# Loading and scoring the first four heads in pairs, and three smaller changes of order

One change to a tuned attention-and-mixer kernel: the first four heads of q and k are loaded, cast, transposed and scored as two pairs, each with its own score sets; V comes behind the next q and k in the load queue; the identity matrix is built first; and some operations get finer urgency levels.

## The chip, the cores and the metric

One core of one Trainium2 chip. The metric is the device time of one execution in microseconds (us). Times are medians of several runs. The kernel before and a variant always ran on the same chip in alternation. "Clock" is the mean clock granted to TensorE, 1.0 being full speed.

## The reference

```python
# q, k, v: (8 batches, 8 heads, 576 positions, 64); the mask is causal in blocks of 64
scores = scale * q @ k^T                        # masked, softmax over the last axis
x = (softmax(scores) @ v), heads side by side   # (8, 576, 512)
h = relu(x^T @ w_tok1) @ w_tok2                 # token mixing: 576 -> 256 -> 576
u = x + h^T
out = u + relu(u @ w_ch1) @ w_ch2               # channel mixing: 512 -> 1536 -> 512
```

## The kernel before

The kernel writes every operation into a list with an engine, a planned cost, the operations it waits for and a priority; its own list scheduler plans the whole run with these costs and then emits the instructions of each engine in the planned order. The order on an engine is thus fixed when the kernel is built, from planned times.

The first four heads: k and q, 128 partitions (four heads of 32 rows each), in two column halves, one on SyncE's queue and one on ScalarE's. Casts and transposes take all 128 partitions at once. Everything after these loads comes through GpSimd's queue.

```python
def load_qk(b, hg, after=[]):
    first = b == 0 and hg == 0
    ...
    for n, (src, raw, dst) in enumerate(((k, kraw[i], kT[i]), (q, qraw[i], qT[i]))):
        ...
        for f, (k0, k1) in enumerate(parts):             # two column halves
            if first:
                def emit_load(o, ...):
                    queue = nc.sync if o.engine == "SP" else nc.scalar
                    queue.dma_start(out=st[:, D * k0 : D * k1], in_=hbm[:, D * k0 : D * k1])
                ld = P.add(("SP", "ACT")[f % 2], 0.45, emit_load, (), -1e4 + n, xfer=(k1 - k0) * 0.1)
                ...
                ld = P.add(EVAC, {"ACT": act_cost(w), "DVE": dve_cost(w)}, emit_cast, [ld], -1e4 + 2 + n)
            ...                                          # then a transpose on VectorE
```

Products of zeros are there to keep TensorE's clock up while there is no work: 16 at the start, and up to 110 small ones that the scheduler drops into whatever TensorE idle time it plans between 5 and 20 us.

```python
def raise_clock():
    def emit(o, bank=bank):
        for _ in range(WARM):                            # WARM, KEEP = 16, 110
            nc.tensor.matmul(out=bank_of(bank), lhsT=zeros[:, 0:128], rhs=zeros, start=True, stop=True)
    P.add("PE", WARM * 0.36, emit, pads["zeros"], -1e6, take=[(BANK, bank)], give=[bank])
    for n in range(KEEP):
        def emit(o, bank=bank):
            nc.tensor.matmul(out=bank_of(bank)[:, 0:256], lhsT=zeros[:, 0:128], rhs=zeros[:, 0:256], ...)
        P.add("PE", 0.11, emit, pads["zeros"], 1e6, take=[(BANK, bank)], give=[bank],
              at=5.0 + 0.12 * n, until=20.0, quick=True)
```

A score set multiplies k by q for several heads. A head uses 32 of the array's 128 rows (`r = slice(32 * h, 32 * h + 32)`), so a set for two heads has half of the rows in use (the timelines show such a product as `32*128`, one on all rows as `128*128`). Before the change the very first set takes all four heads at once; all others take pairs.

The softmax here doesn't subtract the row's maximum and nothing guards it: scores larger than these inputs give would overflow.

Of the kernel before, what the change touches and what calls it, by code (L numbers as in the profile page):

```python
# [149 lines left out]
def kernel(  # L150
# [96 lines left out]
    def init_tiles():  # L247
        def fill(engine, key, prio, *parts):
            for t, value in parts:
                def emit(o, t=t, value=value):  # L250
                    (nc.vector if engine == "DVE" else nc.gpsimd).memset(t, value)

                pads.setdefault(key, []).append(P.add(engine, 0.17, emit, (), prio))

        for i, t in enumerate(kT):
            fill("DVE", ("kT", i), -1e4 + i, (t[:, S:640, :], 0.0))
        for i in range(2):
            fill(
                "DVE", ("v", i), -60 + 20 * i,
                (v1[i][64:128, 4, :, :], 0.0),  # L260
                (v1[i][:, 0:4, :, 64:65], 1.0),
                (v1[i][0:64, 4, :, 64:65], 1.0),
            )
            fill("DVE", ("e", i), -70, (e_sb[i][:, :, 1536:1600], 0.0))
            fill("DVE", ("et", i), -70, (et_sb[i], 0.0))
            fill("DVE", ("um", i), -70, (um_sb[i], 0.0))
        fill("DVE", "zeros", -1e5, (zeros, 0.0))
        fill("DVE", "w1", -70, (w1_sb[64:128, 4, :], 0.0), (w1o_sb[0:64, :], 0.0))
        fill("DVE", "w2", -70, (w2_sb[:, :, S:640], 0.0))

        def emit(o):
            make_identity(nc, ident)

        pads["ident"] = [P.add("POOL", 0.9, emit, (), 5.5)]

    def raise_clock():

# [30 lines left out]
    def cast(o, dst, src):  # L308
        if o.engine == "ACT":
            nc.scalar.copy(dst, src)  # L310
        else:
            nc.vector.tensor_copy(dst, src)

    def load_qk(b, hg, after=[]):
        i = (2 * b + hg) % 3
        first = b == 0 and hg == 0
        prio = 10 * b + 4 * hg - (100 if b == 0 else 0)
        parts = ((0, NB // 2), (NB // 2, NB))
        done = []
        for n, (src, raw, dst) in enumerate(((k, kraw[i], kT[i]), (q, qraw[i], qT[i]))):  # L320
            hbm = src[b, 4 * hg : 4 * hg + 4].rearrange("h (p k) d -> (h p) (k d)", p=32)
            raw2 = raw.rearrange("p k d -> p (k d)")

            st = stage[0][:, 1152 * n : 1152 * (n + 1)]
            raw_war = reuse(("raw", n, i))
            T_war = reuse(("T", n, i))
            loads = []
            if not first:
                def emit_load(o, hbm=hbm, raw2=raw2):
                    nc.gpsimd.dma_start(out=raw2, in_=hbm)  # L330

                loads = [P.add("POOL", 0.66, emit_load, raw_war, prio + n, xfer=8 * 0.191)]
            for f, (k0, k1) in enumerate(parts):
                if first:
                    def emit_load(o, k0=k0, k1=k1, hbm=hbm, st=st):
                        queue = nc.sync if o.engine == "SP" else nc.scalar
                        queue.dma_start(out=st[:, D * k0 : D * k1], in_=hbm[:, D * k0 : D * k1])

                    ld = P.add(("SP", "ACT")[f % 2], 0.45, emit_load, (), -1e4 + n, xfer=(k1 - k0) * 0.1)

                    def emit_cast(o, k0=k0, k1=k1, raw2=raw2, st=st):
                        cast(o, raw2[:, D * k0 : D * k1], st[:, D * k0 : D * k1])

                    w = D * (k1 - k0)
                    ld = P.add(EVAC, {"ACT": act_cost(w), "DVE": dve_cost(w)}, emit_cast, [ld], -1e4 + 2 + n)
                    reads(("g", 0), ld)
                    loads = [ld]

                def emit(o, raw2=raw2, dst=dst, k0=k0, k1=k1):
                    nc.vector.transpose(  # L350
                        dst[:, 0:S, :]
                        .rearrange("p s e -> p (s e)")
                        .bitcast(I32)
                        .rearrange("p (a k) -> p k a", k=NB)[:, k0:k1],
                        raw2.bitcast(I32).rearrange("p (k a) -> p k a", k=NB)[:, k0:k1],
                    )

                op = P.add("DVE", 0.02 + 32 * (k1 - k0) * 0.00185, emit, loads + T_war + after, prio + 0.1 * n, urgent=-(b > 1))
                reads(("raw", n, i), op)
                done.append(op)  # L360
        return done

    def load_v(b):

        t = v1[b % 2]
        war = reuse(("v", b % 2))
        staged = b < 2
        done = [[], []]
        for hg in range(2) if b == 0 else (None,):
            hs = slice(0, H) if hg is None else slice(4 * hg, 4 * hg + 4)  # L370
            nh = hs.stop - hs.start
            for J in range(5):
                p = 128 if J < 4 else 64
                st = stage[1][0:p, DM * J : DM * (J + 1)].rearrange("p (h d) -> p h d", h=H)[:, hs]
                dst = t[0:p, J, hs, 0:64]

                def emit(o, J=J, p=p, hs=hs, dst=st if staged else dst):
                    src = v[b, hs, 128 * J : 128 * J + p, :].rearrange("h p d -> p h d")
                    nc.gpsimd.dma_start(out=dst, in_=src)  # L379

                prio = (10 * b + (0, 5.7, 6)[min(b, 2)] if b else (-95.5, 2)[hg]) + 0.01 * J
                sw = reuse(("gs", J)) if staged and b else [] if staged else war
                op = P.add("POOL", 0.2 + 0.075 * nh, emit, sw, prio, xfer=p * nh / 16 * (0.0175 if staged else 0.0145))
                if staged:
                    def emit(o, st=st, dst=dst):
                        cast(o, dst, st)

                    op = P.add("DVE", dve_cost(64 * nh, 2), emit, [op] + war, 10 * b + 2 if b else -94)
                    reads(("g", 1), op)
                    reads(("gs", J), op)  # L390
                for g in (0, 1) if hg is None else (hg,):
                    done[g].append(op)
        return done
# [190 lines left out]
    def first_attention(ready, v_ready):  # L584
# [3 lines left out]
        for j in range(4):  # L588
# [6 lines left out]
            for n, s in enumerate((2, 1, 0)):  # L595
                width = sum(w for _, _, _, w in SETS[s])
                parts = tuple((hg,) + r for r in SETS[s])
                dst = e[:, hs, 512 * s : 512 * s + width]
                if j == 0 and n == 0:

                    note = {}
                    early = [{}, {}]
                    op = score_set(
                        0, parts, range(4), ready[hg], prio - 0.05, [(SC, note)] + [(BANK, x) for x in early]
                    )
                if j == 1 and n == 0:
                    these = []
                    for h, x in zip(heads, early):
                        def emit(o, h=h, x=x, e=e):
                            nc.scalar.activation(e[:, h, 1024:1536], bank_of(x), EXP, scale=scale)  # L610

                        these.append(P.add("ACT", act_cost(512), emit, [op0], prio, give=[x], urgent=2))
                else:
                    if j or n:
                        note = {}
                        op = score_set(0, parts, heads, ready[hg], prio + 0.1 * n, [(SC, note)])
                    else:
                        op0 = op
                    these = [exp(dst, width, op, note, prio + 0.1 * n, urgent=2)]
                if n == (1 if j else 2):  # L620
                    tails = first_tail(hg, heads, [op] + ready[hg], prio + 0.1 * n + 0.05)
                exps += these
                for c in MASKS[s]:
                    exps.append(mask(e, c, hs, these, prio, urgent=1))
            for h in heads:
                deps = exps + v_ready[hg] + pad + pads["e", hg]
                done.append(head_out(0, 4 * hg + h, deps, -2900 + j, tails[h], urgent=1))
        return done

    def attention(b, ready, v_ready):  # L630
# [82 lines left out]
    def first_uT(x_done, a_done, w2_ready):  # L713
# [3 lines left out]
        for m in range(NDM):  # L717
# [24 lines left out]
                        stop=(t == NDT - 1),  # L742
                    )

            op = P.add("PE", mm_cost(512, 2), emit, [a_done[m], first] + w2_ready, -2700 + m, urgent=1)
            reads(("a", 0), op)
            reads(("x", 0), op)

# [4 lines left out]
                else:  # L753
                    nc.vector.tensor_copy(uT[0][:, :, m, :], ps)

            done.append(P.add(EVAC, evac_cost(512), emit, [op], -2700 + m, give=[bank], urgent=1))
        return done

    def token_mix(b, x_done, w1_ready, w2_ready):
# [9 lines left out]
        u_done, done, um_done = [], [], []  # L769
        if b == 0:  # L770
            a_all = [
                token_up(0, slice(128 * m, 128 * m + 128), (0, 1), x_done[2 * m : 2 * m + 2], [], w1_ready, -2800 + m, 1)
                for m in range(NDM)
            ]
            done = first_uT(x_done, a_all, w2_ready)
# [245 lines left out]
    warm_up()  # L1021
    qk = {}
    vv = {}
    qk[0, 0] = load_qk(0, 0)
    qk[0, 1] = load_qk(0, 1, qk[0, 0])
    vv[0] = load_v(0)
    init_tiles()
    raise_clock()
# [3 lines left out]
    for b in range(B + 1):  # L1032
        if b < B:
            if b > 0:
# [1 line left out]
                    qk[b, hg] = load_qk(b, hg)  # L1036
                vv[b] = load_v(b)
            x_done[b] = (
                attention(b, (qk[b, 0], qk[b, 1]), vv[b]) if b else first_attention((qk[0, 0], qk[0, 1]), vv[0])
            )  # L1040
        if b > 0:
            p = b - 1
# [44 lines left out]
```

## Time and profile before

| | before |
|---|---|
| time, median of 3 | 308.61 us (308.06 to 310.44) |
| profiled run: time, span, clock | 309.31, 307.5 us, 1.0 |
| TensorE busy | 98% of the span |
| first exponential on ScalarE | 10.58 us |
| first channel-up product | 29.04 us |

The prediction below shows the lines that carry the argument. Two more are needed later. The first is TensorE's timeline at the start (start, duration, engine, line, operation, output from input, shapes, count, and in brackets the idle time ahead and what ended it):

```profile
1.20 5.60 PE L282 MATMUL mm<-zeros 128*128 128x512 bf16 x16 [1.20 <-DVE zeros L251]
6.63 1.58 PE L289 MATMUL mm<-zeros 128*128 128x256 bf16 x13
9.91 0.32 PE L465 MATMUL sc<-qT,kT 32*128 32x320 bf16 x2 [1.70 <-DVE qT L350]
```

Thirteen of the small zero products stand between the first sixteen and the first scores. TensorE is idle 1.70 us all the same, because q landed later than planned. The profile's clock row misses one thing here: the first sixteen start 0.42 us apart up to 5.2 us and 0.22 us apart after it, so TensorE begins at half speed, and the trace's clock records begin only at 5.2 us. All 15 traces begin like this, up to some point between 3.84 and 6.86 us. "Clock 1.0" and "never" below leave this start out.

The second is the chain of waits, here two long pieces of it (start, duration, what):

```profile
29.10 2.71 PE mm L879 x12
...
291.20 12.99 PE mm L963 x72
```

They are the first and the last long stretch of channel mixing; their starts are the marks for the comparison.

### The profile page before, as it was taken

The numbers are of one execution on the slowest core, as the hardware profiler recorded it, in microseconds if no ns is written. First come the engines' busy times: TensorE is split into PE (matmuls) and PEld (weight loads), VectorE is DVE, ScalarE is ACT, GpSimd is POOL, SyncE is SP. The second block draws the span as 40 slices with busy tenths as digits, with TensorE's granted clock in tenths as the row PEclk, the third lists the DMA queues.
The fourth block names the chain that finished last, engine by engine and source line by source line (L and its number), as shares of the span: only waits on it lengthen the run. The fifth ranks groups of instructions, "written<-read, shape, count | busy, mean of one in ns | idle before, by whom it ended". The sixth has DMA issues, their size and how long they took to land.

```text
span 307.5 us, 7211 instructions
## 1 busy us (share of the span) xinstructions
PE 300.9 (98%) x3036; PEld 162.0 (53%) x3036; DVE 158.0 (51%) x396; ACT 165.6 (54%) x235; POOL 62.3 (20%) x96
## 2 busy tenths in 40 slices
PE   8799999999999999999999999999999999999995
PEld 3466447464564545545545556555445644545643
DVE  5677738997875859866749634362033012011022
ACT  3796774657775576785566784515405602604600
POOL 7865435620511241320050000000000000000000
PEclk9999999999999999999999999999999999999999
DMA  7999999997695599995292005112321312111013
GB/s 237 187 183 208 214 216 184 230 192 175 85 138 81 113 186 119 137 94 54 85 79 87 2 18 53 70 68 54 60 76 71 68 68 80 24 68 70 0 34 137
DMA packets 55872, 33.13 MB, mean 108 GB/s; under 512 B 43872, under 2 KB 46048, under 8 KB 55840
## 3 DMA queue, kind: packets, MB, share of 16 engines
q0 software_dynamic: 35808, 18.52, 45.8%
q1 hardware_dynamic: 19744, 13.57, 17.1%
q10 hardware_dynamic: 288, 0.59, 0.5%
q8 instruction: 23, 0.38, 0.5%
q14 instruction: 9, 0.07, 0.1%
HBM read 35.85 MB, written 9.44 MB: 147 GB/s over the span
## 4 chain that ended last, share of the span: by engine, by line
PE 93%; DMA 2%; ACT 2%; DVE 1%; issue 1%; ACTq 0%
PE mm L963 31%; PE mm L879 28%; PE mm L512 10%; PE sc L465 9%; PE mm L693 6%; PE mm L787 5%; PE mm L906 4%; DMA gT<-in_q_dram 2%; DVE qT L350 1%; ACT e_sb L484 1%; PE mm L737 1%; ACT uT L855 0%; PE mm L955 0%; PE mm L722 0%; ACT qraw L310 0%
## 5 line engine op out<-in xcount | busy, mean ns | idle before, releaser
L484 ACT ACTIVATE e_sb<-sc 128x1024 bf16<-128x1024 f32 x95 | 92.5, 1027 | 33.2 <-PE sc L465 32.4
L879 PE MATMUL mm<-uT,wc_sb 128*128 128x512 bf16 x384 | 88.8, 380 | 0.2 <-ACT uT L855 0.2
L963 PE MATMUL mm<-wc_sb,gT 128*128 128x512 bf16 (+1 forms) x396 | 88.6, 373 | 0.0
L679 ACT ACTIVATE gT<-mm 128x512 bf16<-128x512 f32 x75 | 44.9, 598 | 64.7 <-PE mm L879 63.7
L879 PEld LDWEIGHTS <-wc_sb 128*128 128x128 bf16 x384 | 42.2, 114 | 39.7 <-issue 3.7
L963 PEld LDWEIGHTS <-gT 128*128 128x128 bf16 x396 | 37.0, 98 | 41.8 <-issue 3.6
L988 DVE TENSOR_TENSOR o_sb<-mm,u_sb 128x512 f32<-128x512 f32 (+1 forms) x29 | 19.5, 672 | 63.2 <-PE mm L963 63.2
L465 PE MATMUL sc<-qT,kT 32*128 32x320 bf16 (+4 forms) x744 | 35.5, 281 | 1.9 <-DVE qT L350 1.7
L512 PEld LDWEIGHTS <-e_sb 128*128 128x128 bf16 x896 | 30.8, 97 | 8.1 <-issue 4.3
L512 PE MATMUL mm<-v,e_sb 128*128 128x65 bf16 x896 | 33.2, 193 | 0.0
L540 DVE TENSOR_TENSOR x_sb<-mm,rinv 128x320 bf16<-128x320 f32 x64 | 30.5, 488 | 1.8
L379 POOL DMA_DIRECT2D v<-in_v_dram x30 | 25.3, 861 | 29.0 <-PE sc L465 21.6
L465 PEld LDWEIGHTS <-kT 32*128 32x128 bf16 x752 | 12.3, 93 | 20.8 <-issue 18.1
L350 DVE STREAM_TRANSPOSE qT<-qraw 128x288 int32<-128x288 int32 x32 | 21.5, 705 | 2.1 <-ACT qraw L310 1.9
L350 DVE STREAM_TRANSPOSE kT<-kraw 128x288 int32<-128x288 int32 x32 | 20.4, 706 | 3.2 <-PE sc L465 2.3
L808 DVE TENSOR_TENSOR u_sb<-mm,x_sb 128x512 bf16<-128x512 f32 x28 | 17.6, 685 | 5.8 <-PE mm L787 5.7
L681 DVE TENSOR_SCALAR gT<-mm 128x512 bf16<-128x512 f32 x21 | 14.5, 689 | 11.3 <-PE mm L879 11.0
L490 DVE MEMSET e_sb<- 64x128 uint32 (+1 forms) x72 | 10.5, 153 | 17.8 <-ACT e_sb L484 15.1
L693 PE MATMUL mm<-x_sb,w_sb 128*128 128x512 bf16 (+1 forms) x102 | 18.1, 317 | 0.0
L787 PE MATMUL mm<-aT,w_sb 128*128 128x512 bf16 x72 | 17.7, 380 | 0.0
L330 POOL DMA_DIRECT2D kraw<-in_k_dram x15 | 8.4, 558 | 36.7 <-DVE kT L350 20.2
L534 DVE RECIPROCAL rinv<-mm 128x5 f32<-128x5 f32 x64 | 11.3, 184 | 6.5 <-PE mm L512 6.1
(66 smaller groups left out, 186.4 us busy)
## 6 DMA issues: line engine op xcount, KB each, us to landing
out_dram<-o_sb SPq DMA_DIRECT2D x15, 512.0 KB, 2.8
kraw<-in_k_dram POOLq DMA_DIRECT2D x15, 288.0 KB, 7.6
qraw<-in_q_dram POOLq DMA_DIRECT2D x15, 288.0 KB, 7.5
v<-in_v_dram POOLq DMA_DIRECT2D x24, 128.0 KB, 5.4
wc_sb<-in_moe_w_ch_dram POOLq DMA_DIRECT2D x8, 192.0 KB, 7.5
wc_sb<-in_moe_w_ch_dram POOLq DMA_DIRECT2D x3, 512.0 KB, 10.6
out_dram<-o_sb SPq DMA_DIRECT2D x10, 128.0 KB, 2.4
gT<-in_v_dram POOLq DMA_DIRECT2D x9, 128.0 KB, 7.1
```

The source lines that it names most:

```text
L350: nc.vector.transpose(dst[:, 0:S, :] .rearrange("p s e -> p (s e)") .bitcast(I32) .rearrange("p (a k) -> p k a", k=NB)[:, k0:k1], raw2.bit ...
L379: nc.gpsimd.dma_start(out=dst, in_=src)
L465: nc.tensor.matmul(out=home(n)[:, c0 : c0 + w], lhsT=kT[i][r, j0 : j0 + 128, par], rhs=qT[i][r, i0 : i0 + w, par], start=(par == 0), stop= ...
L484: nc.scalar.activation(dst, sc[SC.index(note["pool"])][:, :, 0:n], EXP, scale=scale)
L512: nc.tensor.matmul(out=u[:, I, 0:65], lhsT=w, rhs=vt[:, J, head, 0:65], start=(J == 0), stop=(J == I),)
L540: nc.vector.tensor_tensor(out=xt[:, :, 64 * head : 64 * head + 64], in0=u[:, :, 0:64], in1=ri.to_broadcast([128, 5, 64]), op=MULT,)
L679: nc.scalar.activation(dst, src, RELU)
L693: nc.tensor.matmul(out=bank_of(bank)[:, w * n : w * n + w], lhsT=wt[:, tt : tt + 255 : 2], rhs=xt[:, c, cols], start=(c == 0), stop=(c == 4),)
L787: nc.tensor.matmul(out=bank_of(bank), lhsT=w2_sb[:, t, c0 : c0 + 128], rhs=at[:, t, :], start=(t == 0), stop=(t == NDT - 1),)
L879: nc.tensor.matmul(out=bank_of(bank), lhsT=wc1_sb[:, m, channels(cc)], rhs=uT[b % 2][:, :, m, :], start=(m == 0), stop=(m == NDM - 1),)
L963: nc.tensor.matmul(out=ps, lhsT=gt[:, cc, c0 : c0 + 128], rhs=wc2_sb[:, cc, cols], start=(cc == 0 and not turned), stop=(cc == NDC - 1),)
L988: nc.vector.tensor_tensor(out=dst, in0=ps, in1=(ut if mixed else ut[:, si, :])[:, cols], op=ADD)
```

## The change

The intent: the first exponential needs only two heads, so load, cast, transpose and score two heads first and let the other two follow. The other edits take work out of the way of this start, or order what follows it. Cut to its core:

```diff
-        pads["ident"] = [P.add("POOL", 0.9, emit, (), 5.5)]
+        pads["ident"] = [P.add("POOL", 0.6, emit, (), -1e6)]
...
+    def load_first_qk():
+        for f in range(2):                               # two pairs of heads
+            rows = slice(64 * f, 64 * f + 64)
+            for n, (src, raw, dst) in enumerate(((k, kraw[0], kT[0]), (q, qraw[0], qT[0]))):
+                hbm = src[0, 2 * f : 2 * f + 2].rearrange("h (p k) d -> (h p) (k d)", p=32)
+                if f == 1:
+                        nc.sync.dma_start(out=st[rows], in_=hbm)
+                    whole = [P.add("SP", 0.45, emit_load, (), prio, xfer=NB * 0.05)]
+                for c in range(2):
+                    if f == 0:
+                            queue.dma_start(out=st[rows, cols], in_=hbm[:, cols])
+                        loads = [P.add(("SP", "ACT")[c], 0.45, emit_load, (), prio, xfer=half * 0.05)]
+                    ...                                  # cast and transpose of 64 partitions
...
-                prio = (10 * b + (0, 5.7, 6)[min(b, 2)] if b else (-95.5, 2)[hg]) + 0.01 * J
+                prio = (10 * b + (0, 5.7, 6)[min(b, 2)] if b else (-94.9, 2)[hg]) + 0.01 * J
...                                                      # every score set takes a pair of heads
-                done.append(head_out(0, 4 * hg + h, deps, -2900 + j, tails[h], urgent=1))
+                done.append(head_out(0, 4 * hg + h, deps, -2900 + j, tails[h], urgent=1.3))
...                                                      # other levels: 1 -> 1.1 and 1.2
```

The planned transfer times are `* 0.05` where the kernel before has `* 0.1`.

## The prediction

> **What bounds the kernel now.** I read the engine table and the 40 slices first, then the chain of waits of the first 31 us, then the busy times by stage, last the timelines of VectorE and of the POOL queue around what the chain pointed at.
>
> ```profile
> PE 300.9 (98%) x3036; PEld 162.0 (53%) x3036; DVE 158.0 (51%) x396; ACT 165.6 (54%) x235; POOL 62.3 (20%) x96
> PE   8799999999999999999999999999999999999995
> PEclk9999999999999999999999999999999999999999
> ```
>
> TensorE is busy from one end to the other, at the full clock, so the time is TensorE's work plus what it loses. But part of the early work is not work: in the first 17 us the kernel slips in 46 matmuls on zeros that only keep TensorE's clock up. Real matmuls run without gaps only from the first channel-up matmul (29.04 us); what the change can win, it wins by bringing that point, and all after it, forward. The chain of the front says what sets it:
>
> ```profile
> 1.18 6.67 DMA gT<-in_q_dram
> 7.87 0.68 ACT qraw L310
> 8.57 1.30 DVE qT L350 x2
> ...
> 10.58 0.48 ACT e_sb L484
> ```
>
> The second q load lands at 7.84 us; cast, two transposes and the first score set follow, and the first exp starts at 10.58. From there ScalarE is solid for 12.1 us (eleven exps at 0.91 us start to start, two halves at 0.48, eight tails at 0.10) up to 22.7; then 6.3 us of value products, token-up, token-down and casts lead to 29.04.
>
> The stage table (stretch, length, busy PE, PEld, DVE, ACT, POOL, clock, DMA share, GB/s) shows a second bound:
>
> ```profile
> 2.00:5.00 3.00, 3.00 (x8) 1.06 (x7) 2.04 (x13) 1.45 (x3) 3.00 (x5) 1.00 0.98 355
> 12.00:14.00 2.00, 1.92 (x26) 1.01 (x22) 1.12 (x4) 2.00 (x6) 1.96 (x4) 1.00 0.71 142
> 18.00:28.00 10.00, 10.00 (x178) 7.48 (x177) 7.98 (x28) 7.73 (x16) 4.56 (x10) 1.00 1.13 201
> 28.00:38.00 10.00, 10.00 (x79) 4.50 (x77) 6.84 (x12) 8.25 (x11) 5.28 (x8) 1.00 1.09 214
> 38.00:48.00 10.00, 10.00 (x106) 4.82 (x105) 3.90 (x12) 6.70 (x10) 4.02 (x6) 1.00 1.10 214
> ```
>
> The DMA engines are full (share 1 and over) from 2 us to 48 us, except around 12 to 14. And at the end of that stretch TensorE meets them, in VectorE's and TensorE's timelines:
>
> ```profile
> 45.78 0.43 DVE L312 CAST v<-gT 128x512 bf16<-128x512 f32 x1 [1.33 <-DMA gT<-in_v_dram]
> 46.56 0.42 DVE L312 CAST v<-gT 64x512 bf16<-64x512 f32 x1 [0.35 <-DMA gT<-in_v_dram]
> ```
> ```profile
> 47.28 0.59 PE L512 MATMUL mm<-v,e_sb 128*128 128x65 bf16 x14
> ```
>
> The last piece of V of batch 1 lands at 46.53, its cast ends at 46.98, and the first product with it starts at 47.28. So TensorE's slack against this transfer is 47.28 - 46.98 = about 0.3 us. This is my main point: the front may be shortened by microseconds, but TensorE reaches this product at most 0.3 us sooner unless the transfer itself lands sooner.
>
> [...] the first packet of the POOL queue starts at 4.83, 3.6 us after its first issue (1.25). [...] The kernel before loads 128 partitions at 355 GB/s (row 2:5)[...]. [...] for 8.83 to 18.05: POOL issues back to back (0.74 us for a V piece, 0.53 for others) and the DMA share falls to 0.71.
>
> **The change, part by part.** I compared the built programs. After the front the TensorE order is the same, matmul for matmul, to the end, and the real matmuls are equally many (46 zero matmuls become 35). So the whole effect is when the front ends, and whether the data keep up.
>
> 1. *First pair.* Before: 1.18 MB must land before the first score. After: heads 0 and 1 alone, 0.59 MB, in four DMAs of 0.15 MB on the two queues. At 355 GB/s from about 1.9 us it has moved at 3.6; landings came some 0.9 us behind the bytes (k: 0.59 MB moved by about 3.65, landed 4.5 to 4.7), so 4.5. [...]
> 2. *Casts and transposes.* 64 partitions cost as much as 128: the length of a row is the same. Four casts at 0.58 us start to start, now all on ScalarE (2.3 us), then the last transpose (0.7). [...]
> 3. *A new wait.* In ScalarE's new order three casts of the second pair stand before the first exp. Its q lands last of the 1.18 MB: 6.2 at the full rate[...]. So the first exp starts between about 8.0 and 9.6 instead of 10.58: 1.0 to 2.6 us sooner. Middle: 1.8.
> 4. *Score sets.* Twelve exps of 0.91 in place of eleven and two halves: 12 x 0.91 against 11 x 0.91 + 2 x 0.48, so 0. The VectorE pieces keep: cast and transposes of pair two must end before ScalarE's fourth exp, some 3 us after the first. No loss.
> 5. *Identity first.* 0.55 us of POOL work goes from 13.73 to the start; the first POOL load is issued at 1.8 instead of 1.25 and its packets could start at 5.4, when the SP and ACT loads end anyway. No loss while those run at 355 GB/s; later 0.55 us are free.
> 6. *V behind q/k of the other four heads.* V of heads 0 to 3 lands about 1.3 us later, ahead of its need (the first product stood at 14.84). But from the ninth POOL load on, each waits for the landing of the one eight before. Before, the tenth waited for a V piece (landed 9.35); after, it waits for q, the second in the queue, which by the bytes ahead of it lands near 10. The issues behind, V and the 512-byte packets of the token weights, move 0 to 0.7 us later in an issue-bound stretch.
> 7. *Urgency levels.* They reorder AV, token-up and token-down within the 6.3 us after the last exp; TensorE has the same work there. 0 to 0.2 us.
>
> The sum by the front alone: 1.8 us sooner at 29.04. Against it, the transfers: the POOL queue must move about 7.9 MB (its 36 loads up to V of batch 1, counted as written: 0.29 MB a q or k, 0.13 a half piece of V, 0.20 and 0.52 the channel weights) before the batch-1 product; the change removes no byte, and from 14 us on that queue is saturated. Its shift at V of batch 1 is the shift of steps 5 and 6: between 0.4 us sooner and 0.7 us later at the full rate[...]. Middle: 0.2 us later. So TensorE arrives 1.8 us sooner at this product and waits about 1.7 us: net gain 0.3 - 0.2 = 0.1 us, 308.5.
>
> **The rivals.** *A: the front's gain stays.* If V of batch 1 lands 1 us or more sooner, because the gap at 12 to 14 us (1.3 us of idle DMA: 4 us between 10 and 14 at share 0.75 instead of 1.1) is filled, the time is 306.5 to 307. For it: identity no longer splits the issues, and the front has been tuned with transfers in mind. Against: the eight-deep rule, the back-to-back issues. [...] *C: q and k of batch 1.* q of its first heads landed at 25.37 and needs 1.3 us of transposes; the score set stood at 28.47. This caps the front's gain at 1.8 us, but V caps it lower.
>
> **Range and chances.** The net is the smaller of the front's gain (1.0 to 2.6) and 0.3 us plus the transfer's shift (-1.0 to +0.4). I give that seven parts in ten, centred on 308.5; rival A gets three, near 306.9. Together: 308.2 us, from 306.7 to 309.5 in 8 cases of 10. Over 2% means 6.2 us, three times what the front could give: 0.02 for faster, and 0.01 for slower.
>
> **What would show it.** First exp at 8.0 to 9.6 us; the first channel-up matmul at about 27.2; V of batch 1 landing at 46.1 to 47.3; TensorE idle by over 1 us just before the first product of batch 1; afterwards the same timeline as before, shifted by less than 0.5 us. I am wrong if that product starts at 46 us or sooner: then POOL's queue was not the bound I take it for. I am wrong the other way if the SP and ACT loads still run at 7.5 us, or if the first exp is no sooner than 10.

Passages that rest on figures which no trace here showed are cut, and with them terms of the forecast's sum, all from a lower rate for loads of 64 partitions: a second, later landing in steps 1 to 3, a later shift of V of batch 1, and rival B, which gave 309.5. Step 2 without them: q at 4.5, last cast 6.2, transpose 6.9, scores 7.5. The late ends that are left in the ranges (9.6 and 1.0 in step 3, and so its middle of 1.8; -1.0 in the transfer's shift) come from the cut terms and were not shown by a trace then. The sum came to this: 1.8 us sooner at the front, of which the wait for V of batch 1 leaves 0.3 - 0.2 = 0.1 us, so 308.5; with rival A 308.2. What the runs showed later of that rate stands under e7.

Two statements stand there without their figures. Step 2, casts of 64 and of 128 partitions: two take 1.25 us either way (e3, e4). Step 6, loads that wait for the one eight before: in the trace of the kernel before, GpSimd's ninth load was issued at 8.83 us, after 1.97 us of idleness that ended with the landing of the first; the idleness ahead of the 23rd to the 26th and of the 29th to the 32nd (0.29 to 0.93 us) ended each time with the landing of a load of the tensor that stands eight before. And one figure went with its cut passage: in 2 to 5 us SyncE's queue moved 0.53 MB and ScalarE's 0.52.

## The result, and the profile after

| | before | after |
|---|---|---|
| time, median of 6 | 308.34 us (307.83 to 310.44) | 320.75 us (320.36 to 321.84) |
| ratio | | 1.0401 (95%: 1.0366 to 1.0435) |
| clock, mean of the span | 1.0 | 0.963 (0.961 to 0.968 in all six) |
| first exponential | 10.58 | 13.80 |
| first channel-up product | 29.04 | 40.68 |

A ratio is the mean time of one kernel's fast runs over that of the other's fast runs of the same rounds, so it isn't quite the ratio of the medians quoted. All six runs after count as fast ones: the low clock is this kernel's own and not the chip's slower state.

The kernel is 4% slower. Where the time went can be read off the chain of waits. Its first long piece is a DMA, then the same two marks as before:

```profile
2.91 10.18 DMA gT<-in_q_dram
40.75 2.71 PE mm L894 x12
...
302.88 12.94 PE mm L978 x71
```

40.75 - 29.10 = 11.65 and 302.88 - 291.20 = 11.68: from the first channel-up product to the end the two kernels run alike. All of the loss lies ahead of it. There, two things are new. The first stands in the row of slices, which in the kernel before was nines throughout:

```profile
PEclk9555999999999999999999999999999999999999
```

Each digit is one fortieth of the span, 8 us. In three of them TensorE had about half its clock. The second is in the table by stage (stretch, length, busy PE, PEld, DVE, ACT, POOL, clock, DMA share, GB/s):

```profile
2.00:5.00 3.00, 3.00 (x8) 1.06 (x7) 2.43 (x14) 2.67 (x4) 3.00 (x6) 1.00 0.92 206
```

In this stretch the DMA engines are nearly as busy as before (share 0.92 against 0.98) but move 206 GB/s against 355. TensorE's and ScalarE's timelines show what follows from each:

```profile
1.19 5.91 PE L282 MATMUL mm<-zeros 128*128 128x512 bf16 x16 [1.19 <-DVE zeros L251]
10.19 1.89 PE L498 MATMUL sc<-qT,kT 32*128 32x320 bf16 x16 [3.09 <-DVE qT L353]
11.85 0.33 PE L595 MATMUL mm<-qT,kT 32*128 32x64 bf16 x4
12.12 1.46 PE L289 MATMUL mm<-zeros 128*128 128x256 bf16 x6
14.88 1.03 PE L498 MATMUL sc<-qT,kT 32*128 32x512 bf16 x4 [1.30 <-ACT e_sb L517]
```
```profile
8.72 0.67 ACT L310 CAST qraw<-gT 64x576 bf16<-64x576 f32 x1 [2.33 <-DMA gT<-in_q_dram]
10.85 1.24 ACT L310 CAST kraw<-gT 64x576 bf16<-64x576 f32 x2 [1.46 <-DMA gT<-in_k_dram]
13.11 0.67 ACT L310 CAST qraw<-gT 64x576 bf16<-64x576 f32 x1 [1.01 <-DMA gT<-in_q_dram]
13.80 1.02 ACT L517 ACTIVATE e_sb<-sc 128x1024 bf16<-128x1024 f32 x1
```

The thirteen zero products ahead of the first scores are gone: in the plan the pair arrives so early that TensorE has no idle time there. In truth it is idle 3.09 us. Six zero products come back behind the first set, and then 1.30 us are idle again. The first scores were ready by 12.2 us, but on ScalarE the three casts of the second pair stand ahead of the first exponential in program order, and the last of them waits for a q that lands at 13.09.

Following the clock in steps of half a microsecond, it falls at 9.24 us (within 0.05) and comes back at 33.1, 23.9 us later. These rows have the columns of the table by stage:

```profile
5.75:9.10 3.35, 1.35 (x6) 0.48 (x5) 0.84 (x2) 1.02 (x2) 2.04 (x3) 1.00 1.08 250
16.15:19.45 3.30, 3.30 (x27) 1.36 (x25) 2.29 (x9) 1.84 (x2) 3.30 (x7) 0.50 1.11 136
29.80:33.05 3.25, 3.25 (x48) 2.32 (x46) 1.48 (x5) 2.09 (x4) 2.08 (x4) 0.50 1.16 210
33.20:36.60 3.40, 3.36 (x76) 3.10 (x74) 2.08 (x8) 0.77 (x2) 2.86 (x4) 1.00 1.09 217
```

Two riddles are in them. The fall follows a stretch in which TensorE was busy 40% of the time. And TensorE is busy without a gap from 14.9 us on, yet the clock doesn't come back for another 18 us.

Two theories, then. *Clock*: most of the loss is TensorE at half speed, because the zero products are gone. *Loads*: most of it is the late q of the second pair; the clock is a by-product. The rivals within each: which gap counts and what brings the clock back; and whether the loads are slow because 64 partitions are slow or because GpSimd's queue takes the engines.

### The profile page after: what moved, and what is told of

Its sections match the earlier page's. It is cut to its first block, busy times and chain, and to the rows that moved or that the text cites. A ratio compares the mean times of both kernels' runs of the same rounds, so it can differ in the third digit from the quotient of the medians.

```text
span 319.0 us, 7175 instructions
## 1 busy us (share of the span) xinstructions
PE 307.7 (96%) x2995; PEld 165.0 (52%) x3025; DVE 159.8 (50%) x401; ACT 168.6 (53%) x237; POOL 62.3 (20%) x96
## 4 chain that ended last, share of the span: by engine, by line
PE 93%; DMA 3%; issue 1%; ACT 1%; SPq 1%; DVE 1%; DVEq 0%
PE mm L978 29%; PE mm L894 27%; PE sc L498 11%; PE mm L545 10%; PE mm L708 5%; PE mm L802 5%; PE mm L921 3%; DMA gT<-in_q_dram 3%; PE mm L289 1%; SPq L338 0%; PE mm L752 0%; ACT uT L870 0%; ACT e_sb L517 0%; DVE x_sb L573 0%; PE mm L970 0%
## 5 line engine op out<-in xcount | busy, mean ns | idle before, releaser
L517 ACT ACTIVATE e_sb<-sc 128x1024 bf16<-128x1024 f32 x96 | 93.8, 1022 | 36.9 <-PE sc L498 36.4
L978 PE MATMUL mm<-wc_sb,gT 128*128 128x512 bf16 (+1 forms) x378 | 85.8, 373 | 1.5 <-issue 0.8
L498 PE MATMUL sc<-qT,kT 32*128 32x64 bf16 (+4 forms) x752 | 41.0, 297 | 4.4 <-DVE qT L353 3.1
L545 PEld LDWEIGHTS <-e_sb 128*128 128x128 bf16 x896 | 32.7, 100 | 9.0 <-issue 5.2
L545 PE MATMUL mm<-v,e_sb 128*128 128x65 bf16 x896 | 35.1, 197 | 0.0
L498 PEld LDWEIGHTS <-kT 32*128 32x128 bf16 x752 | 13.6, 96 | 25.5 <-issue 21.4
L383 DVE STREAM_TRANSPOSE kT<-kraw 128x288 int32<-128x288 int32 x30 | 19.2, 707 | 2.5 <-PE sc L498 2.3
L383 DVE STREAM_TRANSPOSE qT<-qraw 128x288 int32<-128x288 int32 x30 | 20.0, 704 | 0.2
```

The lines of the kernel that those rows point to most:

```text
L383: nc.vector.transpose(dst[:, 0:S, :] .rearrange("p s e -> p (s e)") .bitcast(I32) .rearrange("p (a k) -> p k a", k=NB)[:, k0:k1], raw2.bit ...
L498: nc.tensor.matmul(out=home(n)[:, c0 : c0 + w], lhsT=kT[i][r, j0 : j0 + 128, par], rhs=qT[i][r, i0 : i0 + w, par], start=(par == 0), stop= ...
L517: nc.scalar.activation(dst, sc[SC.index(note["pool"])][:, :, 0:n], EXP, scale=scale)
L545: nc.tensor.matmul(out=u[:, I, 0:65], lhsT=w, rhs=vt[:, J, head, 0:65], start=(J == 0), stop=(J == I),)
L978: nc.tensor.matmul(out=ps, lhsT=gt[:, cc, c0 : c0 + 128], rhs=wc2_sb[:, cc, cols], start=(cc == 0 and not turned), stop=(cc == NDC - 1),)
```

## The experiments

Thirteen kernels ran, and all gave correct results. All runs but one, told below, were fast ones. The kernel before ran beside them on the same chip (308.17 us in the first batch, 308.29 in the second, 308.47 in the third, 308.37 and 308.64 for the last two). Three points of time tell most of each; the last column is when the clock was at half speed in the profiled run.

| run | median us | ratio | first exp | first channel-up | half clock |
|---|---|---|---|---|---|
| e1 before, no zeros ahead of the scores | 307.83 | 0.9994 | 8.84 | 27.67 | never |
| e2 after, all gaps filled with zeros | 314.14 | 1.0188 | 13.11 | 34.28 | never |
| e3 after, loads as before | 309.79 | 1.0061 | 9.22 | 28.47 | never |
| e4 before, identity first | 309.42 | 1.0044 | 9.05 | 27.54 | never |
| e5 before, scores 1.6 us later | 309.33 | 1.0025 | 10.44 | 28.89 | never |
| e6 the same, and no zeros ahead of them | 310.51 | 1.0069 | 11.16 | 30.41 | 10.25 to 13.7 |
| e7 after, GpSimd's loads held back | 316.40 | 1.0251 | 9.14 | 36.12 | 16.0 to 29.7 |
| e8 after, loads and identity as before | 309.28 | 1.0024 | 9.40 | 28.69 | never |
| e9 after, first gap filled | 320.16 | 1.0388 | 13.61 | 39.89 | 17.0 to 34.1 |
| e10 after, more zeros behind the first gap | 314.31 | 1.0184 | 13.17 | 33.90 | 9.15 to 16.0 |
| e11 before, levels and V's place only | 309.17 | 1.0027 | 9.20 | 27.70 | never |
| e12 pairs alone | 309.41 (fast: 309.18) | 1.0026 | 9.20 | 28.90 | never |
| e13 e10 with zeros of 64 rows | 322.49 | 1.0443 | 13.45 | 41.81 | 10.3 to 34.2 |

### e1: the zero products ahead of the first scores, taken out of the kernel before

```diff
+                kept.append(0)
+                for _ in range(len(kept) > 13):          # the first 13 are left out
                     nc.tensor.matmul(... zeros ...)
```

> The kernel before, with the 13 zero matmuls ahead of its first scores left out, so that TensorE is idle from 6.8 to 9.9 us (3.1 us, as long as the gap in the changed kernel) and nothing else differs. Clock theory: the granted clock falls to half at about 8.6 us, stays there for some 20 us, the first channel-up matmul comes 5 to 9 us late and the time is 313 to 318 us. Load rival (the changed kernel lost its 12 us to late loads, the clock is a by-product that costs nothing): 308.3, within 1 us.

Measured: 307.83 us, ratio 0.9994 (0.9975 to 1.0012), clock 1.0. It didn't test what it was made for. In this run q landed at 6.27, not at 7.84 as in the profiled run before, so TensorE's gap was only 1.88 us. What follows is two smaller things: a gap of 1.88 us here didn't cost the clock (more on this behind e13), and the profile of the kernel before, with its first exponential at 10.58, had caught a late landing; 8.8 to 9.1 us is more usual (e1, e4). The run also is no better than the kernel before: the interval includes 1.

### e2: every gap of the changed kernel filled with zeros

```diff
-            for _ in range(WARM):
+            for _ in range(30):
...
+                for _ in range(5 if len(kept) <= 6 else 3 if len(kept) <= 11 else 1):
                     nc.tensor.matmul(... zeros ...)
```

> The changed kernel with zero matmuls in TensorE's gaps (30 in place of 16 before the first scores, 5 for 1 and 3 for 1 in the next two gaps); order of all else unchanged. Clock theory: clock 1.00 throughout, first exp still near 13.8 us, first channel-up matmul at about 32 us instead of 40.7, time 311.5 to 313. Load rival: the front is set by the loads and ScalarE, so 318 to 321.

Measured: 314.14 us, clock 1.0 throughout, first exponential at 13.11, nearly as late as in the changed kernel. The loss is 6.0 us (314.14 - 308.17) in place of 12.4 (320.75 - 308.34). So keeping the clock is worth 6.4 us, and the other half of the loss has nothing to do with it. The time lies between the two expected ranges: neither theory alone carries it all.

### e3 and e4: the loads, and the identity

```diff
 # e3: after, the first loads as in the kernel before
-                hbm = src[0, 2 * f : 2 * f + 2].rearrange("h (p k) d -> (h p) (k d)", p=32)
+                hbm = src[0, 0:4].rearrange("h (p k) d -> (h p) (k d)", p=32)
...
-                            queue.dma_start(out=st[rows, cols], in_=hbm[:, cols])
+                            queue.dma_start(out=st[:, cols], in_=hbm[:, cols])
...
-                        loads = [P.add(("SP", "ACT")[c], 0.45, emit_load, (), prio, xfer=half * 0.05)]
+                        both[n, c] = [P.add(("SP", "ACT")[c], 0.45, emit_load, (), prio, xfer=half * 0.1)]
 # e4: before, and only
-        pads["ident"] = [P.add("POOL", 0.9, emit, (), 5.5)]
+        pads["ident"] = [P.add("POOL", 0.6, emit, (), -1e6)]
```

> The changed kernel with the first loads as before (four DMAs of 128 partitions on two queues); casts, transposes and score sets still in pairs. The list scheduler then puts 13 zero matmuls back ahead of the first scores by itself. If the 64-partition loads are what made the data late: q lands by about 6 to 8 us instead of 8.7 and 13.1, first exp at 9.5 to 10.5, clock at full speed, time 307 to 309. If the POOL queue that now starts sooner is what made them late (its packets share the engines), q still lands after 9 us and the time is over 310.

> The kernel before with only the identity moved to the front of the POOL queue. If POOL's packets, 0.5 us later, leave the engines to the SP and ACT loads: q lands at about 6.5 to 7.5 instead of 7.84, 0.3 to 1 us gained in the front, and by the transfer bound (0.3 us of slack at V of batch 1) no more than 0.5 us in the time: 307.8 to 308.5. If the packets start sooner, as in the changed kernel (3.65 instead of 4.83), q lands later, 8.5 or more, and the time is 309 or more.

e3: 309.79 us, ratio 1.0061, clock 1.0. With the old loads (and their old planned time) the scheduler itself puts the 13 zero products back, so this one edit cures both the loads and the clock: from e2, which has only the clock cured, the loads are worth 314.14 - 309.79 = 4.35 us. But the first exponential is at 9.22, no sooner than in e1 and e4, though q landed at 6.09 and 6.28. ScalarE's timelines say why, e3 first, then e4:

```profile
6.11 1.25 ACT L310 CAST qraw<-gT 64x576 bf16<-64x576 f32 x2
7.39 0.67 ACT L310 CAST kraw<-gT 64x576 bf16<-64x576 f32 x1
7.96 1.24 ACT L310 CAST qraw<-gT 64x576 bf16<-64x576 f32 x2
9.22 1.02 ACT L511 ACTIVATE e_sb<-sc 128x1024 bf16<-128x1024 f32 x1
```
```profile
6.33 1.25 ACT L310 CAST qraw<-gT 128x576 bf16<-128x576 f32 x2 [0.26 <-DMA gT<-in_q_dram]
9.05 1.94 ACT L484 ACTIVATE e_sb<-sc 128x1024 bf16<-128x1024 f32 x2 [1.47 <-PE sc L465]
```

A cast of 64 partitions takes as long as one of 128 (two take 1.25 us either way). So two pairs need twice the casts, and those of the second pair, three on ScalarE (7.39 to 9.22), take up the 1.5 us in which ScalarE had waited for the scores, and a little more. The pair's head start is spent on the second pair's casts.

e3 also shows the wait that the prediction made its main point, in TensorE's timeline:

```profile
47.14 0.19 PE L539 MATMUL mm<-v,et_sb 128*128 128x65 bf16 x1 [0.55 <-DVE v L312]
```

TensorE waits 0.55 us for the cast of the last piece of V of batch 1, which landed at 46.56 (45.25 in e1).

e4: 309.42 us, ratio 1.0044 (1.0027 to 1.0062). The identity first costs 1.25 us by itself, although the front is not later (first channel-up 27.54 against 27.67 in e1). The loss comes behind it, with waits of 0.83, 0.25 and 0.32 us on TensorE between 61 and 67 us, where the kernel before has one of 0.18. Some transfers are later: the last big piece of token weights landed at 19.07 (18.28 before, 17.85 in e1). V of batch 1, at 45.84, is later than in e1 (45.25) but not than in the kernel before (46.53). Moving one operation on GpSimd also put a piece of V of batch 2 ahead of a k load in the queue. What made those waits isn't settled.

### e5 and e6: a gap in the kernel before, and its control

```diff
 # both: the first scores about 1.6 us later
+                        for _ in range(3 if late else 0):
+                            nc.scalar.copy(idle, zeros)      # 128x512, ahead of a cast of q
 # e6 only: the 13 zero products left out, as in e1
```

> The kernel before with three dummy ScalarE copies of 128x512 ahead of the cast of q, so that the first scores come about 1.6 us later, all 13 zero products still ahead of them. The control for the next run. If only the delay counts: 308.2 plus 1.0 to 1.7 = 309.2 to 309.9 us, clock 1.00 throughout, TensorE idle under 2 us before the first scores. If a later start of the scores as such made the change slow, more than 2 us.

> The same delay, and the 13 zero products ahead of the first scores left out, so that TensorE is idle some 3.4 us (6.3 to 9.7) at full-speed loads. Theory of the clock: as after the change (3.1 us idle), the granted clock falls to half within the next 4 us and stays there for some 20 us, and the kernel takes 4 to 8 us more than the control, 313 to 318 us, mean clock about 0.96. Rival (the clock in the changed kernel fell for another reason, such as the smaller products of its paired scores, or its loads): the clock stays at 1.00 and the time is that of the control within 0.6 us.

e5: 309.33 us, clock 1.0, TensorE idle 1.03 us ahead of the scores. e6: 310.51 us, clock 0.994, idle 2.55 us. Without the zeros the clock did fall, at 10.25 us, with the first loads on 128 partitions and no pair anywhere, so here the gap of 2.55 us, in place of e5's 1.03, was enough to bring it down. But it cost 1.2 us (310.51 - 309.33) and not the expected 4 to 8, and the clock came back after only 3.4 us. TensorE's gap and the table of stretches of e6:

```profile
10.14 0.40 PE L471 MATMUL sc<-qT,kT 32*128 32x320 bf16 x2 [2.55 <-DVE qT L356]
```
```profile
6.90:10.20 3.30, 0.75 (x8) 0.25 (x9) 1.55 (x4) 2.38 (x5) 2.20 (x3) 1.00 1.10 239
10.30:13.60 3.30, 3.30 (x37) 1.77 (x33) 2.63 (x10) 2.43 (x3) 3.23 (x7) 0.50 1.11 212
13.70:17.00 3.30, 3.17 (x59) 2.10 (x52) 1.31 (x6) 2.72 (x8) 3.30 (x7) 1.00 1.11 138
```

TensorE was fully busy in the half-speed stretch, as in the changed kernel from 14.9 us on. There it wasn't enough; here it was. In e6 that stretch holds the set of all four heads, which has all rows of the array in use, and seven zero products of 128 rows. In the changed kernel the sets take pairs.

### e7: GpSimd's loads held back

```diff
 # cut: the identity's planned cost rises from 0.6 to 1.45, so that the plan holds GpSimd back too
+                if b == 0 and n == 0:                    # wait for q of the second pair
+                    nc.gpsimd.tensor_copy(held[64:128], stage[0][64:128, 2303:2304])
                 nc.gpsimd.dma_start(out=raw2, in_=hbm)
```

> The changed kernel with GpSimd's first load held back until the last pair's q has landed. Theory A (the pairs' q landed at 13.1 us because the GpSimd queue's packets, from 3.7 us on, took the engines): the last q lands 3 us or more earlier, at 8 to 10 us, the first exponentials start by 10.8 us, the gap before the first scores shrinks below 2.6 us, and the time falls to 311 to 317 us, though the other four heads come later. Theory B (loads of 64 partitions run at half rate whoever else loads): with 1.18 MB at about 206 GB/s from 2 us on, the last q lands at 7.8 us at the earliest; if it lands after 11 us in spite of an idle GpSimd queue, the half rate alone explains the delay.

Measured: 316.40 us. The last q landed at 8.42 in place of 13.09, and the first exponential started at 9.14. So theory A holds for 4.7 us of the delay, and theory B for what is left: alone on the DMA engines, loads of 64 partitions moved 232 GB/s in 2 to 5 us (343 in e3, whose first loads are of 128 partitions; so 0.68 of that rate), and their last q is still 2.1 us later than the 6.28 of e3. Part of these 2.1 us may have another cause: the second pair comes through one queue and is issued at 2.25 and 2.89, where e3 issues everything on two queues by 1.21; no run separates the two. The first gap was mostly GpSimd's traffic too: the late half of the first pair's q landed at 5.88 in place of 8.70, and TensorE's gap ahead of the first scores was 0.59 us in place of 3.09. The share that GpSimd's queue took in the changed kernel shows in its DMA queues between 4 and 8 us (packets, MB, share of 16 engines):

```profile
q0 software_dynamic: 229, 0.49, 72.4%
q1 hardware_dynamic: 118, 0.33, 27.2%
```

q0 is GpSimd's queue, q1 SyncE's, the one that carried the second pair. The time fell by only 4.35 us against the changed kernel, because the next four heads now came late: TensorE waited for them, and the clock fell there instead, at 16.0 us.

```profile
16.33 0.87 PE L501 MATMUL sc<-qT,kT 32*128 32x320 bf16 x6 [2.13 <-DVE qT L386]
```

### e8, e11 and e12: what is left of the loss

```diff
 # e8: e3, and the identity back
-        pads["ident"] = [P.add("POOL", 0.6, emit, (), -1e6)]
+        pads["ident"] = [P.add("POOL", 0.9, emit, (), 5.5)]
 # e11: the kernel before, and only (cut; the other levels likewise)
-                prio = (... if b else (-95.5, 2)[hg]) + 0.01 * J
+                prio = (... if b else (-94.9, 2)[hg]) + 0.01 * J
-                done.append(head_out(0, 4 * hg + h, deps, -2900 + j, tails[h], urgent=1))
+                done.append(head_out(0, 4 * hg + h, deps, -2900 + j, tails[h], urgent=1.3))
 # e12: e8, and the lines of e11 the other way round
```

> The changed kernel with its first loads as before the change (128 partitions on two queues) and the identity back in its old place; casts, transposes and scores of the pairs, the later V and the levels stay as changed. If the identity's place is what was left of the loss in the run with the old loads (309.8): 308.2 to 308.9 us. If the pairs, the later V or the levels cost it: 309.4 to 310 us, with V of batch 1 landing at about 46.5 us and TensorE idle for it. If the changed parts that are left gain something once the loads are as before: below 307.8 us.

> The kernel before with only the changed urgency levels and the later place of V in the queue: no pairs, no new loads, identity as before. If these carry the 1.0 us that was left in the run with the old loads and the identity back (309.28 against 308.29): 309 to 309.7 us. If the pairs carry it (twice the casts and transposes ahead of the first scores): 307.9 to 308.6 us. Granted clock 1.00 either way.

> Pairs alone: casts, transposes and score sets of the first four heads in pairs, with the loads, the identity, the place of V and the urgency levels all as in the kernel before. With the levels and V's place back, what was 309.28 against 308.29 should become, if these carry the rest of the loss (they alone measured 309.17 against 308.47): 308.0 to 308.7 us, ratio 0.999 to 1.001. If the pairs themselves (eight casts and eight transposes ahead of the last pair's scores in place of four) cost about as much: 309 to 309.8 us. If the pairs gain what the change hoped for once nothing else is in the way: below 307.7 us, and this would be the best version.

e8: 309.28 us, 1.0 us over the kernel before by the medians, but ratio 1.0024 (0.9996 to 1.0053), so not clear of noise. e11: 309.17, ratio 1.0027 (1.0003 to 1.0051). e12: 309.41, ratio 1.0026 (1.0002 to 1.0050); one of its six runs, 314.96 us at clock 0.977, counts as slow because it is over 1.5% above the fastest, and is left out of the ratio (the median of the five fast ones is 309.18). It was not profiled. Its lost clock (0.023 of 312.9 us, 7.2 us, so some 14 us at half speed) would also fit a fall of this kernel's own, four steps of 3.4 us long, so that pairs alone can lose the clock now and then is not excluded. So the first of e12's three expectations fell: the pairs alone cost about as much as pairs and levels together. Neither part gains, each costs 0.2 to 0.3% alone, and together they don't cost the sum. In e12 the loss is in the front (first channel-up 28.90 against 27.67 in e1), in e11 behind it (first channel-up 27.70). With intervals of half a per cent I leave the last 1.0 us at that: none of these small differences is explained. No version beat the kernel before.

### e9 and e10: which gap, and what brings the clock back

```diff
 # e9: after, 14 more zeros ahead of everything
-            for _ in range(WARM):
+            for _ in range(30):
 # e10: after, 16 as they were, and the first 11 of the later ones doubled
+                for _ in range(2 if len(kept) <= 11 else 1):
                     nc.tensor.matmul(... zeros ...)
```

> The changed kernel with 30 zero products ahead of everything in place of 16, nothing else: 14 more of 0.216 us fill 3.0 of the 3.1 us before the first scores. If that gap is what brings the clock down: it stays at 1.00, and the time is that of the run in which all gaps were filled, 313 to 315.5 us. If what follows would bring it down anyway (a second gap of 1.3 us; products of 32 rows, two at a time): it falls to half by 20 us, and the time stays at 318 to 321 us.

> The changed kernel with its gap before the first scores left as it is, and the first 11 of the later zero products doubled. If the clock comes back as soon as a stretch of 3.4 us is dense with 128-row products (as in the kernel before with the late gap, where it came back after 3.4 us): it falls at 9.2 us as in the changed kernel and is back at 16 to 20 us in place of 33, mean clock 0.98 to 0.99, time 314.5 to 317.5 us. If the clock's return has nothing to do with what TensorE does in these stretches: back at 33 us again, and the time 320 to 322 us.

e9: 320.16 us, the same as the changed kernel within 0.6 us. My first idea, that the gap of 3.1 us is the cause, fell. That gap is filled, but the next one, between the six zeros behind the first set and the first exponential's release of its bank, took its place:

```profile
11.60 0.83 PE L289 MATMUL mm<-zeros 128*128 128x256 bf16 x6
14.68 0.63 PE L498 MATMUL sc<-qT,kT 32*128 32x512 bf16 x4 [2.25 <-ACT e_sb L517]
```
```profile
10.30:13.60 3.30, 2.13 (x28) 1.33 (x27) 1.45 (x3) 1.91 (x3) 1.57 (x3) 1.00 1.07 204
13.70:17.00 3.30, 2.32 (x25) 1.10 (x26) 3.18 (x8) 3.30 (x6) 3.30 (x6) 1.00 1.03 171
17.15:20.45 3.30, 3.30 (x24) 1.00 (x20) 2.99 (x15) 2.74 (x5) 2.80 (x6) 0.50 1.02 136
```

The clock fell at 17.0 us, 2.4 us after that gap had ended, at the end of a stretch in which TensorE was busy for 70% of the time, mostly with pairs of 32 rows.

e10: 314.31 us. The first gap stands (2.90 us), the clock falls at 9.15 as before, and eleven more zero products bring it back at 16.0:

```profile
11.88 2.74 PE L292 MATMUL mm<-zeros 128*128 128x256 bf16 x12
14.55 1.03 PE L501 MATMUL sc<-qT,kT 32*128 32x512 bf16 x4
15.52 1.47 PE L292 MATMUL mm<-zeros 128*128 128x256 bf16 x10
```
```profile
12.60:15.90 3.30, 3.30 (x16) 1.51 (x15) 2.60 (x7) 3.00 (x6) 3.30 (x6) 0.50 0.94 177
16.05:19.40 3.35, 3.35 (x38) 1.70 (x37) 2.22 (x9) 2.40 (x3) 3.35 (x7) 1.00 1.12 130
```

Eleven products of no use, at most 2.4 us of TensorE (11 by 0.21, start to start at half clock), make the kernel 6.4 us faster (320.75 - 314.31): as much as preventing the fall altogether in e2. The fall itself costs little (1.2 us in e6 against e5, where it lasts one time 3.41 us); what costs is that it lasts seven times as long.

### e13: the same zeros on half of the rows

```diff
+                rows = slice(0, 64 if len(kept) <= 11 else 128)
-                        lhsT=zeros[:, 0:128], rhs=zeros[:, 0:256],
+                        lhsT=zeros[rows, 0:128], rhs=zeros[rows, 0:256],
```

> The run with the doubled later zero products (314.31 us, clock back at 16.0 us), with those first 22 zero products on 64 rows of the array in place of 128: as many, as long, TensorE as busy. If the clock's return asks only that TensorE be busy for a stretch of 3.4 us: back at 16 us, time 313.5 to 315 us. If it asks for rows in use (the paired score sets use 32 rows twice): not back at 16 us, but only with the value products at 26 to 33 us, mean clock 0.96 to 0.975, time 318.5 to 322 us.

Measured: 322.49 us. As many zero products as in e10, as long, in the same places, and the clock comes back at 34.2 us in place of 16.0:

```profile
12.37 2.74 PE L293 MATMUL mm<-zeros 64*128 64x256 bf16 x12
15.04 1.03 PE L502 MATMUL sc<-qT,kT 32*128 32x512 bf16 x4
```
```profile
13.75:17.05 3.30, 3.30 (x17) 1.47 (x16) 3.19 (x9) 2.81 (x5) 3.30 (x6) 0.50 1.00 165
17.15:20.45 3.30, 3.30 (x24) 1.41 (x24) 0.75 (x4) 1.02 (x1) 2.58 (x5) 0.50 1.05 140
```

Set beside e10's rows: the same shares of zeros and scores in the stretch (72% and 28%, from the starts of the products in the trace), the same full business, and the only difference is 64 rows for 128. So a busy TensorE wasn't enough here: twenty-two zero products of 128 rows brought the clock back after 6.8 us, the same of 64 rows after 23.9.

All six half-speed times are, within 0.1 us, whole multiples of 3.41 us: 1 (e6), 2 (e10), 4 (e7), 5 (e9), 7 (after, e13). Cutting each run into such windows from its fall, and taking the share of a window in which products of 128 rows ran, the clock came back after windows of 0.69 (e13), 0.72 (after, e10) and 1.0 (e7, e9), and, in e6, 0.47 with the four-head set in the rest; it did not after 0.61 (e9) or after 0.44 and less (after), though TensorE had no gap in most of these either.

The same cut says more of the fall than the gap's length does. In each of the 15 traces the clock records change only at whole steps of 3.41 us from the first rise, and that rise comes at another moment from run to run. In the window just before the fall TensorE was busy 22% (e13), 25% (e6), 37% (after), 38% (e10) and 47% (e7) of the time. Where the clock stayed up, the emptiest window of the first 35 us had 61% (e1): the border at 7.63 us splits its gap of 1.88 us. e9 doesn't fit busy time alone: the clock stayed after a window of 65% and fell after the next, of 69%. By gaps alone the clock fell with gaps of 3.09 (after), 2.90 (e10), 2.84 (e13), 2.55 (e6) and 2.13 us (e7), and in e9 2.4 us after one of 2.25 had ended; it didn't fall with 1.88 (e1), 1.70 (before) and 1.03 (e5). So what exactly brings the clock down was not settled, and where the windows lie, which differed from run to run (first rise between 3.84 and 6.86 us), may have a part in it. One unprofiled run of the kernel before (310.18 us, clock 0.994, in e13's batch) has about one half-speed window too.

The clock records of the changed kernel's trace show the two values and the steps: 1.00 for 3.413 us from the first rise, 0.50 for 23.893 us, which is seven times that, then 1.00 to the end.

## Why the prediction was wrong

I predicted 308.2 us (306.7 to 309.5) and gave "slower" one chance in a hundred; it was 320.75. In terms of the runs, the 12.4 us divide like this, as differences of the losses of the runs, each within about 1 us: clock 6.4 (after to e2, or to e10), first loads 4.4 (e2 to e3), the identity's place 0.6 (e3 to e8, not clear of noise; 1.25 alone in e4), pairs and levels 1.0 (e8, not clear of noise).

**The step that failed first is the sentence ahead of the sum: "So the whole effect is when the front ends, and whether the data keep up."** It took TensorE's clock as given. The prediction had even counted that "46 zero matmuls become 35" and said what they are for, and then gave their loss no price. The 13 that vanished (later ones make up for two of them) stood ahead of the first scores, in the planned idle time that the plan's cheaper loads had taken away. In their place came 3.09 us of idleness, then half a clock for 23.9 us. This term was not in the sum, and it is half of the loss. The prediction also read the clock row as full speed from one end to the other, where the first 4 to 7 us of every trace run at half.

**Step 1, the first pair's landing (4.5 at 355 GB/s).** Of the four loads k landed at 3.68 and 4.44, half of q at 5.70, the other half at 8.70. With GpSimd's queue held back (e7) the two halves landed at 5.59 and 5.88, so 1.1 to 1.4 us of the delay stand without GpSimd's traffic, and the contention, 2.8 us, was missing. The rate was lower: 206 GB/s between 2 and 5 us, which includes the first packets of GpSimd's queue, and 232 alone in e7, against the 343 (e3) to 355 (before) of 128 partitions.

**Step 3, the new wait, was right in kind and far off in size.** ScalarE did wait for the second pair's casts. Their q was to land at 6.2 at 355 GB/s; it landed at 13.09. e7 splits this: 8.42 with GpSimd's loads out of the way, at 232 GB/s in 2 to 5 us, and 4.7 us more of contention. I had let GpSimd's packets begin at 5.4, "when the SP and ACT loads end anyway"; they began in number at 3.65 (in the kernel before the first one started at 4.83), and then took 0.49 MB of 0.84 between 4 and 8 us; what decides when they begin was not tested. The two queues got no even split either: 229 packets to SyncE's 118; why was not tested. And the gain itself wasn't there: with fast loads (e3, e12), and with pair loads that nothing disturbs (e7), the first exponential started at 9.14 to 9.22, no sooner than 8.84 to 9.05 in e1 and e4. The second pair's casts, or in e7 the wait for its q, take ScalarE's old wait. Also, the 10.58 that I measured the gain from was one run's late landing.

**Step 4, score sets (0), was right at full clock:** in e3 the twelve exponentials take 12.06 us (9.22 to 21.28), against 12.1 before. **Step 5, identity first ("no loss"), was wrong** by 1.25 us, measured in e4. **Steps 6 and 7** (V later by 0 to 0.7 us, levels 0 to 0.2): together 0.7 us in e11, with 0.1 to 1.6 in the interval, so right as far as the interval tells. The issue-bound stretch that step 6 leans on (8.83 to 18.05) holds only to 14 us: the DMA share was 0.71 from 12 to 14, but from 14 to 18 it was 1.18 with GpSimd still issuing back to back.

**The main point, that V of batch 1 takes the gain back,** was not tested by the change itself, whose front was 11.6 us late: V landed at 49.02, 2.5 us later than before, and its first product stood at 58.92. e3 shows that the wait is real (0.55 us) where the front is nearly as early as before. **Rival B** (slower loads of 64 partitions, 309.5) had the right cause for about a third of the loss and a size too small, some 1 us where the loads cost 4.4, because it left out the contention and the casts' wait. **Rival A** and the favourable half of the range had no ground: the front didn't gain. (Their weights, seven and three parts of 308.5 and 306.9, make 308.0 and not 308.2.)

What I said would prove me wrong did: "if the SP and ACT loads still run at 7.5 us, or if the first exp is no sooner than 10".

## What to carry to other kernels

Filler work that keeps a clock up is part of the kernel's speed (6.4 of the 12.4 us lost here): when a change moves or removes it, price what TensorE does without it, and look at the clock row of the profile before anything else. Here filler on all 128 rows of the array brought the clock back at 16.0 us (e10), on 64 of them it came back only at 34.2 (e13), no sooner than with half as many (33.1, after). If a scheduler places filler by planned times, a load that is planned too fast takes the filler away just where the real wait is. And cutting a first load into smaller ones pays only if the pieces arrive faster and the work on them shrinks as well; here 64 partitions came at a lower rate (232 GB/s alone in e7, 343 for 128 in e3), their casts cost as much as those of 128 (two take 1.25 us either way), and another queue's traffic came in between (0.49 MB of 0.84 between 4 and 8 us).
